# Expert weights: who computes the low half, VectorE behind its own share of a group, or ScalarE and GpSimd behind ScalarE's share

## The chip, the cores and the metric

One core of a Trainium2 chip runs the whole program. The metric is the device time of one execution in microseconds. Beside it the profiler records one execution instruction by instruction; where a text speaks of "the trace", it means that execution.

## What is computed

Three layers follow each other, cut here to what matters.

```python
# 1: attention through 32 packed tokens; batch 8, 8 heads, 576 tokens, head size 64
p_packed = softmax_attention(p, k, v)
x = softmax_attention(q, p_packed, p_packed)          # -> (8, 576, 512)
# 2: Fourier mixing, normalisation and a channel MLP
u = x + real(fft(fft(x, axis=1), axis=2))
x = u + relu(norm(u) @ w_ch1) @ w_ch2                 # 512 -> 2048 -> 512
# 3: mixture of 8 experts, each token goes to one of them
h = relu(x[b, s] @ w1[e])                             # 512 -> 1024
out[b, s] = p[e] * (h @ w2[e])                        # 1024 -> 512
```

The weights `w1` and `w2` come in 32-bit floats. The kernel multiplies in 16-bit floats: each operand is kept as a high half, the value rounded to 16 bits, and a low half, what the rounding lost, and a product is the sum of three passes (high by high, high by low, low by high).

## The kernel before, in words

The program goes through the batch with a software pipeline. `Mix` is the channel MLP of one batch element: 16 groups `f`. In a group, `mm1(f)` makes `hp` with 12 matmuls of 512 columns (L739), ScalarE takes the relu into the high half of `ht` (L746), VectorE makes its low half (L747), and two groups later `mm2` adds 12 more matmuls into `acc` (L759). This is the bulk of TensorE's work. Between the matmuls of a group `tick()` draws steps from background generators: the attention and Fourier part of the next batch element (`attention`, L315 on), the end of the last one (`after_mix`), and `expert_weights`. Two of the Mix runs, R0 and R1, have 256 columns. A scheduler fixes the order of each engine's queue when the program is built, and every engine runs its own queue strictly in that order; a step of the attention that comes late on any engine thus holds TensorE at the matmul that needs it.

`expert_weights` turns 64 blocks `st` (128 x 1024, named `se` in the trace, two buffers) into 128 tiles `so` (128 x 2 x 512, two buffers) of high and low halves and writes them to the scratch tensors `WS1` and `WS2`, from which the third layer loads them. Per tile, `split` scales into the high half on ScalarE (L261) and subtracts on VectorE (L262). SyncE's queue issues the load of `se` (L300) and the write of `so` (L309). This goes on from 176 to 962 us of the trace. `pace[0]` is VectorE's last instruction of the newest group (L747); `tc.issue_after(pace[0])` orders the instructions that the block puts on the same engine behind that one, and makes no wait on another engine.

The steps of attention that come up below, with their lines: `s` (L368), the first scores, in the accumulation buffers `att`, of which there are two; `scores2`, `greatest2` (L498, L500), the exponentials (L504), `sums2` on GpSimd (L509, L510), `divide2` on VectorE (L515 to L518), `fold2` (L525, L526, L530 to L534), `parts2` (`eh`, ScalarE L540, GpSimd L542, for the last third VectorE L544); `channels` k = 0 to 3, matmuls `gp` (L469) that ScalarE (L473) and VectorE (L474) turn into `g`. `lp` (L776), `bp` (L563) and `gp` take turns on the two `att` buffers, so the matmuls of one wait until VectorE has read an earlier one. At the end of a batch element `qs` (L632, ScalarE) and `rl`, `ru` (VectorE, L636 to L658) do the last 32 rows, and `s` of the next element takes the buffer that `ru` leaves. `un`, `unh` and a transposing DMA (L689 to L696) make the next Mix's operand.

Of the kernel before, what the change touches and what calls it, by code (L numbers as in the profile page):

```python
# [11 lines left out]
AF = mybir.ActivationFunctionType  # L12
ALU = mybir.AluOpType
# [140 lines left out]
def build(tc, A, stop=None, manual=False):  # L154
    nc = tc.nc
    with ExitStack() as ctx:
        if manual:
            ctx.enter_context(tc.manual_schedule())
        _build(tc, nc, ctx, A, stop)
# [20 lines left out]
def _build(tc, nc, ctx, A, stop):  # L180
# [72 lines left out]

    U, UT = {}, {}
    wdone = [0]
    pace = [None]
    held = []


    def split(dst_hi, dst_lo, src, scale):  # L260
        nc.scalar.activation(dst_hi, src, AF.Copy, scale=scale)  # L261
        nc.vector.scalar_tensor_tensor(dst_lo, src, scale, dst_hi, ALU.mult, ALU.subtract)  # L262
# [31 lines left out]
    def expert_weights():  # L294
        for e in range(NE):
            for k in range(8):

                st = wp.tile([128, 2, 512], F32, tag="st", name=f"se{e}_{k}", bufs=2)
                src = A["w1"][e, :, k] if k < 4 else A["w2"][e, :, 2 * k - 8:2 * k - 6].rearrange("p a n -> p (a n)")
                nc.sync.dma_start(st.rearrange("p a n -> p (a n)"), src)  # L300
                yield
                for a in range(2):
                    so = wp.tile([128, 2, 512], F16, tag="so", name=f"so{e}_{k}_{a}", bufs=2)

                    with tc.issue_after(pace[0]):
                        split(so[:, 0], so[:, 1], st[:, a], 64.0 if k < 4 else 256.0)
                    yield
                    c0 = 2048 * (k % 4) + 1024 * a
                    nc.sync.dma_start((WS1 if k < 4 else WS2)[e, :, c0:c0 + 1024], so.rearrange("p x n -> p (x n)"))  # L309
                yield  # L310
# [392 lines left out]
    def tick(n=1.0):  # L703
        for it in list(bg):
            if it[0] is ew and phase[0] < EWS:
                continue
            it[1] += it[2] * n
            while it[1] >= 1.0:
                it[1] -= 1.0
                try:  # L710
                    next(it[0])
                except StopIteration:
                    bg.remove(it)
                    break
# [9 lines left out]
    class Mix:  # L724
# [5 lines left out]
        def mm1(self, f):  # L730
            ntok, ut = self.ntok, self.ut
            phase[0] = f
            while wdone[0] <= f:
                next(cw)
            hp = psM.tile([128, 512], F32, tag="h", name=f"hp{self.tiles[0][1]}_{f}")
            n = 0
            for c in range(4):
                for (x, y) in PASS:
                    nc.tensor.matmul(hp[:, :ntok], w1h[:, f, c, x], ut[:, 4 * y + c, :ntok],  # L739
                                     start=n == 0, stop=n == 11)  # L740
                    n += 1
                if c < 3:
                    tick(ntok / 2048)
            ht = wp.tile([128, 2, 512], F16, tag="ht", name=f"ht{self.tiles[0][1]}_{f}", bufs=3)
            with tc.high_priority(offset=URGENT):
                nc.scalar.activation(ht[:, 0, :ntok], hp[:, :ntok], AF.Relu)  # L746
                pace[0] = nc.vector.scalar_tensor_tensor(ht[:, 1, :ntok], hp[:, :ntok], 0.0, ht[:, 0, :ntok],  # L747
                                                         ALU.max, ALU.subtract).ins
            self.hts[f] = ht
            tick(ntok / 2048)  # L750
# [282 lines left out]


    cw, ew = ch_weights(), expert_weights()
    for n, _ in enumerate(attention(0)):
        if n == CW0:
# [207 lines left out]
```

## Time and profile before

| what | value |
|---|---|
| median of three runs | 1516.62 us |
| lowest and highest | 1511.03 and 1521.59 us |
| the profiled execution | 1514.66 us |
| its span, first to last instruction | 1512.9 us |
| TensorE's mean granted clock | 0.971 of full speed |

Predictions start from the profiled execution and end at the median. In the rows of the profile PE is TensorE, DVE is VectorE, ACT is ScalarE, POOL is GpSimd and SP is SyncE; `out<-in` names what an instruction writes and reads, and after a bar stand busy time, the mean duration of one, and the idle time of the engine before it with what ended it.

### The profile page before, as it was taken

To read this page: it belongs to the slowest core of one execution; us is meant where nothing else is said; L and a number is where in the kernel's file an instruction comes from. 1 tells how busy PE (TensorE), PEld (TensorE's weight loads), DVE (VectorE), ACT (ScalarE), POOL (GpSimd) and SP (SyncE) were. 2 spreads that over 40 slices of the span, in tenths; PEclk is the share of its full clock that TensorE was granted. 3 is DMA by queue.
4 is the path that set the end of the run, shared out by engine and by line. 5 is a ranking of instruction groups with operands and counts; after the bars stand their busy time and mean duration, and the time that the engine had idled before them with its cause. 6 is when DMAs were issued, how large, how long until landed. Compare 5 with 4: busy or idle time off the path is not lost. (4 is left out here: it accounts for less than half of the span.)

```text
span 1512.9 us, 28826 instructions
## 1 busy us (share of the span) xinstructions
PE 1403.3 (93%) x11340; PEld 825.5 (55%) x11340; DVE 769.0 (51%) x1615; ACT 460.5 (30%) x858; POOL 278.9 (18%) x296
## 2 busy tenths in 40 slices
PE   4588888998999899999999999999899999999996
PEld 3334434544564454454444456455677677777764
DVE  5789977567655766666766665433531111111110
ACT  3343444344333434434435333111111111111111
POOL 1312113203200420320321220000212121121211
PEclk6689999999999999999999999999999999999998
DMA  8275476386476637647656546244946636783371
GB/s 268 61 226 177 142 190 156 111 208 164 122 166 158 191 108 201 170 118 219 149 131 198 125 124 170 56 180 139 252 114 197 170 89 172 226 245 81 79 230 54
DMA packets 233163, 239.70 MB, mean 158 GB/s; under 512 B 168191, under 2 KB 179583, under 8 KB 232384
## 3 DMA queue, kind: packets, MB, share of 16 engines
q1 hardware_dynamic: 226464, 217.62, 52.6%
q0 software_dynamic: 6560, 20.19, 4.1%
q8 instruction: 91, 1.49, 0.4%
q14 instruction: 48, 0.39, 0.1%
HBM read 267.38 MB, written 53.74 MB: 212 GB/s over the span
## 5 line engine op out<-in xcount | busy, mean ns | idle before, releaser
L759 PE MATMUL acc<-w2h,ht 128*128 128x512 f16 x1728 | 410.3, 379 | 0.8 <-DVE ul L767 0.8
L739 PE MATMUL hp<-ut,w1h 128*128 128x512 f16 x1536 | 371.3, 383 | 5.9 <-DMA ut<-unh 5.2
L739 PEld LDWEIGHTS <-w1h 128*128 128x128 f16 x1920 | 183.7, 98 | 187.8 <-issue 21.0
L759 PEld LDWEIGHTS <-ht 128*128 128x128 f16 x1728 | 165.7, 98 | 185.2 <-issue 6.6
L1107 PE MATMUL ehp<-xgt,w1b 128*128 128x128 f16 x3936 | 232.6, 219 | 3.3 <-DMA w1b<-WS 2.2
L1107 PEld LDWEIGHTS <-w1b 128*128 128x128 f16 x3936 | 225.2, 98 | 15.5 <-DMA w1b<-WS 2.6
L1115 DVE SCALAR_TENSOR_TENSOR hx<-ehp,hx 128x512 f16<-128x512 f32 x82 | 56.6, 691 | 339.3 <-ACT hx L1114 335.5
L1125 PE MATMUL eo<-w2b,hx 128*128 128x512 f16 x984 | 219.2, 379 | 0.0
L747 DVE SCALAR_TENSOR_TENSOR ht<-hp,ht 128x512 f16<-128x512 f32 (+1 forms) x160 | 101.3, 633 | 165.9 <-ACT ht L746 165.7
L1125 PEld LDWEIGHTS <-hx 128*128 128x128 f16 x984 | 94.3, 98 | 106.3
L261 ACT ACTIVATE so<-se 128x512 f16<-128x512 f32 x128 | 79.8, 628 | 194.6 <-DMA WS<-so 154.6
L746 ACT ACTIVATE ht<-hp 128x512 f16<-128x512 f32 (+1 forms) x160 | 87.2, 546 | 138.6 <-PE hp L739 133.5
L1114 ACT ACTIVATE hx<-ehp 128x512 f16<-128x512 f32 x82 | 48.9, 597 | 185.9 <-PE ehp L1107 185.9
L262 DVE SCALAR_TENSOR_TENSOR so<-se,so 128x512 f16<-128x512 f32 x128 | 98.2, 776 | 10.7 <-ACT so L261 10.7
L1133 POOL DMA_INDIRECT out<-ys,sidx x41 | 41.5, 1013 | 332.2 <-ACT ys L1132 310.8
L1132 ACT ACTIVATE ys<-eo,scl 128x512 f32<-128x512 f32 x41 | 28.2, 687 | 179.2 <-PE eo L1125 179.2
L344 POOL TENSOR_TENSOR qh<-q,qh 128x1420 f16<-128x1420 f32 x12 | 34.6, 2880 | 257.3 <-ACT qh L343 233.9
L1075 POOL DMA_INDIRECT xg<-XS,gidx x41 | 42.2, 1029 | 174.9 <-DVE sidx L1031 103.9
L368 PE MATMUL s<-k,p 64*32 64x288 f32 x256 | 24.3, 478 | 24.8 <-DVE ru L648 11.6
L739 PE MATMUL hp<-utr,w1h 128*128 128x256 f16 x384 | 47.1, 272 | 0.0
L563 PE MATMUL bp<-cst,eh 128*128 128x289 f16 (+1 forms) x192 | 33.5, 317 | 13.2 <-ACT eh L540 6.5
L694 POOL TENSOR_TENSOR unh<-un,unh 128x512 f16<-128x512 f32 x32 | 38.6, 1216 | 30.7 <-ACT unh L693 30.7
(288 smaller groups left out, 1346.4 us busy)
## 6 DMA issues: line engine op xcount, KB each, us to landing
w1b<-WS SPq DMA_DIRECT2D x156, 512.0 KB
w2b<-WS SPq DMA_DIRECT2D x156, 512.0 KB
se<-in_w SPq DMA_DIRECT2D x64, 512.0 KB
WS<-so SPq DMA_DIRECT2D x128, 256.0 KB
sw<-in_wc SPq DMA_DIRECT2D x32, 512.0 KB
q<-in_qd SPq DMA_DIRECT2D x16, 710.0 KB
v<-in_vd SPq DMA_DIRECT2D x16, 640.0 KB
k<-in_kd SPq DMA_DIRECT2D x16, 576.0 KB
```

The lines of the kernel that those rows point to most:

```text
L261: nc.scalar.activation(dst_hi, src, AF.Copy, scale=scale)
L262: nc.vector.scalar_tensor_tensor(dst_lo, src, scale, dst_hi, ALU.mult, ALU.subtract)
L739: nc.tensor.matmul(hp[:, :ntok], w1h[:, f, c, x], ut[:, 4 * y + c, :ntok], start=n == 0, stop=n == 11)
L746: nc.scalar.activation(ht[:, 0, :ntok], hp[:, :ntok], AF.Relu)
L747: pace[0] = nc.vector.scalar_tensor_tensor(ht[:, 1, :ntok], hp[:, :ntok], 0.0, ht[:, 0, :ntok], ALU.max, ALU.subtract).ins
L759: nc.tensor.matmul(self.acc[j], ht[:, x, 128 * j:128 * j + 128], w2h[:, f, y], start=f == 0 and n == 0, stop=f == 15 and n == 2)
L1075: nc.gpsimd.indirect_dma_start(out=g_, out_offset=None, in_=XS[0:rows], in_offset=bass.IndirectOffsetOnAxis(ap=gidx[:, b:b + 1], axis=0), ...
L1107: nc.tensor.matmul(hp[:, cols], w1b[b % RB][:, 2 * c + fg, x, cols], xt[b][:, 4 * y + c], start=n == 0, stop=n == 11, skip_group_check=True)
L1114: nc.scalar.activation(ht[:, fg, 0], hp, AF.Relu)
L1115: nc.vector.scalar_tensor_tensor(ht[:, fg, 1], hp, 0.0, ht[:, fg, 0], ALU.max, ALU.subtract)
L1125: nc.tensor.matmul(op, h[:, f // 4, x, 128 * (f % 4):128 * (f % 4) + 128], w2b[b % RB][:, f, y], start=n == 0, stop=n == 23)
L1133: nc.gpsimd.indirect_dma_start(out=A["out"], out_offset=bass.IndirectOffsetOnAxis(ap=sidx[:, b:b + 1], axis=0), in_=ys, in_offset=None, bo ...
```

## The change

For the 128 tiles `so` of the experts' weights the call of `split` is replaced by three instructions. ScalarE scales the 128 x 512 block of `st` in place, in 32 bits; ScalarE copies it into the high half; GpSimd subtracts the high half from the scaled block into the low half. VectorE has no part in it any more. The block is now ordered behind `pace[1]`, ScalarE's relu of the newest group, so ScalarE's two instructions stand behind that relu; GpSimd's one has no such order. `split` stays as it is for the other weights. Line numbers after the change are higher by 2 from there on.

```diff
-    pace = [None]
+    pace = [None, None]
...
-                    with tc.issue_after(pace[0]):
-                        split(so[:, 0], so[:, 1], st[:, a], 64.0 if k < 4 else 256.0)
+                    with tc.issue_after(pace[1]):
+                        nc.scalar.activation(st[:, a], st[:, a], AF.Copy, scale=64.0 if k < 4 else 256.0)
+                        nc.scalar.copy(so[:, 0], st[:, a])
+                        nc.gpsimd.tensor_tensor(so[:, 1], st[:, a], so[:, 0], op=ALU.subtract)
...
-                nc.scalar.activation(ht[:, 0, :ntok], hp[:, :ntok], AF.Relu)
+                pace[1] = nc.scalar.activation(ht[:, 0, :ntok], hp[:, :ntok], AF.Relu).ins
```

The first place is the softmax of attention 5 in groups 7 and 8. On VectorE, before, from the second `g` on (`m_5_2`, `ee_2`, `eo_2` belong to the last third of the rows, `gp_1` to `gp_3` are the channel products):

```order
L474 SCALAR_TENSOR_TENSOR g_6214<-gp_1_6420,g_6214 128x257
L515 TENSOR_REDUCE m_5_2_6354<-t_5_2_6410 99x16
L262 SCALAR_TENSOR_TENSOR so_3_1_6444<-se_3_6345,so_3_1_6444 128x512
L516 TENSOR_SCALAR m_5_2_6354<-m_5_2_6354 99x16
L517 RECIPROCAL m_5_2_6354<-m_5_2_6354 99x16
L518 TENSOR_TENSOR ee_2_6356<-ee_2_6356,m_5_2_6354 99x512
L532 SCALAR_TENSOR_TENSOR eo_2_6451<-ee_2_6356,c_93 99x256
L533 TENSOR_SCALAR eo_2_6451<-eo_2_6451,c_93 99x256
L526 SCALAR_TENSOR_TENSOR ah_2_6447<-ee_2_6356,ah_2_6447 32x512
L474 SCALAR_TENSOR_TENSOR g_6214<-gp_2_6464,g_6214 128x257
```

and after:

```order
L517 TENSOR_REDUCE m_5_2_6424<-t_5_2_6481 99x16
L518 TENSOR_SCALAR m_5_2_6424<-m_5_2_6424 99x16
L519 RECIPROCAL m_5_2_6424<-m_5_2_6424 99x16
L520 TENSOR_TENSOR ee_2_6426<-ee_2_6426,m_5_2_6424 99x512
L534 SCALAR_TENSOR_TENSOR eo_2_6523<-ee_2_6426,c_93 99x256
L528 SCALAR_TENSOR_TENSOR ah_1_6474<-ee_1_6362,ah_1_6474 128x512
L476 SCALAR_TENSOR_TENSOR g_6283<-gp_1_6491,g_6283 128x257
L535 TENSOR_SCALAR eo_2_6523<-eo_2_6523,c_93 99x256
L528 SCALAR_TENSOR_TENSOR ah_2_6519<-ee_2_6426,ah_2_6519 32x512
L546 SCALAR_TENSOR_TENSOR eh_2_6545<-eh_2_6545,c_93,eo_2_6523 99x512
L476 SCALAR_TENSOR_TENSOR g_6283<-gp_2_6536,g_6283 128x257
```

The two tiles `so` are gone from VectorE, and `g` of `gp_1` now stands behind the whole division of `ee_2` and behind `ah_1`; it stood ahead of it. On GpSimd the same stretch, before:

```order
L510 TENSOR_TENSOR t_5_2_6410<-t_5_2_6410 99x16x8
L542 TENSOR_TENSOR eh_0_6400<-eo_0_6383,eh_0_6400 128x512
L542 TENSOR_TENSOR eh_1_6429<-eo_1_6407,eh_1_6429 128x512
L534 TENSOR_TENSOR eo_2_6451<-ee_2_6356 99x256
L387 MEMSET ehl_0_7124 128x2x64
```

and after:

```order
L512 TENSOR_TENSOR t_5_2_6481<-t_5_2_6481 99x16x8
L544 TENSOR_TENSOR eh_0_6471<-eo_0_6453,eh_0_6471 128x512
L308 TENSOR_TENSOR so_3_0_6464<-se_3_6415,so_3_0_6464 128x512
L536 TENSOR_TENSOR eo_2_6523<-ee_2_6426 99x256
L544 TENSOR_TENSOR eh_1_6500<-eo_1_6478,eh_1_6500 128x512
L308 TENSOR_TENSOR so_3_1_6515<-se_3_6415,so_3_1_6515 128x512
```

A subtraction for `so` now stands behind each of the two `eh` instructions.

The second place is the end of attention 5, on ScalarE, where `qs_2` is copied, which `rl` and `ru` on VectorE need; before:

```order
L693 CAST unh_1_1_6875<-un_1_1_6873 128x512
L746 ACTIVATE ht_14_6896<-hp_14_6878 128x512
L261 ACTIVATE so_0_0_6957<-se_0_6944 128x512
L632 COPY qs_2_6929<-P_2_6899 32x257
L261 ACTIVATE so_0_1_6974<-se_0_6944 128x512
```

and after:

```order
L695 CAST unh_1_1_6954<-un_1_1_6952 128x512
L307 CAST so_7_1_6965<-se_7_6927 128x512
L748 ACTIVATE ht_14_6976<-hp_14_6957 128x512
L306 ACTIVATE se_0_7024<-se_0_7024 128x512
L634 COPY qs_2_7009<-P_2_6979 32x257
L307 CAST so_0_0_7037<-se_0_7024 128x512
```

Ahead of `qs_2` stood the making of a tile `so`; now the scaling of the loaded block stands there, and the copy of an earlier block stands ahead of `ht_14`. TensorE's own queue has the same instructions in both programs. In four batch elements the first scores `s` have moved ahead of two or three of the large matmuls beside them.

## Rows read from the trace of the kernel before

**Rows 1.** Page, part 1: engine, busy us, share of the span, instructions

```profile
PE 1403.3 (93%) x11340; PEld 825.5 (55%) x11340; DVE 769.0 (51%) x1615; ACT 460.5 (30%) x858; POOL 278.9 (18%) x296
```

**Rows 2.** One stretch: length, busy us (count) of PE, PEld, DVE, ACT, POOL; granted clock

```profile
176.00:962.00 786.00, 746.44 (x5067) 386.72 (x5065) 508.84 (x1044) 305.06 (x583) 160.00 (x156) 0.99 0.59 155
```

**Rows 3.** What TensorE waited for, 176 to 962 us: total us, times, longest

```profile
PE lp L776 <- DVE g L474: 8.0, 5, 2.0
PE s L368 <- issue: 7.1, 3, 2.6
PE bp L563 <- DVE g L474: 3.5, 4, 1.2
PE gp L469 <- DVE g L474: 2.9, 3, 1.2
PE s L491 <- ACT pth L448: 2.6, 1, 2.6
PE gp L469 <- DVE ee L500: 2.2, 2, 1.8
PE s L368 <- DVE ru L648: 2.1, 1, 2.1
PE pps L427 <- DVE vhl L416: 2.0, 2, 1.3
```

**Rows 4.** Groups of instructions, 176 to 962 us: busy us, mean ns, idle before

```profile
L262 DVE SCALAR_TENSOR_TENSOR so<-se,so 128x512 f16<-128x512 f32 x128 | 98.2, 776 | 10.7 <-ACT so L261 10.7
L747 DVE SCALAR_TENSOR_TENSOR ht<-hp,ht 128x512 f16<-128x512 f32 (+1 forms) x133 | 82.9, 623 | 131.2 <-ACT ht L746 131.0
L261 ACT ACTIVATE so<-se 128x512 f16<-128x512 f32 x128 | 79.8, 628 | 194.6 <-DMA WS<-so 154.6 <-DVE ee L500 6.4 <-issue 5.5
...
L694 POOL TENSOR_TENSOR unh<-un,unh 128x512 f16<-128x512 f32 x28 | 33.6, 1210 | 28.1 <-ACT unh L693 28.1
...
L504 ACT ACTIVATE ee<-ee 128x512 f32<-128x512 f32 (+1 forms) x18 | 11.2, 622 | 8.1 <-DVE ee L500 8.1
```

**Rows 5.** One line each, 176 to 962 us: duration ns min/median/max

```profile
L747 DVE SCALAR_TENSOR_TENSOR ht<-hp,ht x133: 411/684/693, 177.0 to 959.7; 128x512 f16<-128x512 f32 x101, 128x256 f16<-128x256 f32 x32
L526 DVE SCALAR_TENSOR_TENSOR ah<-ee,ah x18: 672/676/3161, 245.6 to 855.8; 128x512 f16<-128x512 f32 x12, 32x512 f16<-32x512 f32 x6
L516 DVE TENSOR_SCALAR m<-m x18: 131/174/1902, 242.9 to 851.3; 128x16 f32<-128x16 f32 x12, 99x16 f32<-99x16 f32 x6
```

**Rows 6.** VectorE's timeline, attention 5, groups 7 and 8: start us, duration us

```profile
630.05 0.42 DVE L474 SCALAR_TENSOR_TENSOR g<-gp,g 128x257 f16<-128x257 f32 x1
...
631.49 2.54 DVE L262 SCALAR_TENSOR_TENSOR so<-se,so 128x512 f16<-128x512 f32 x1
...
637.18 0.41 DVE L474 SCALAR_TENSOR_TENSOR g<-gp,g 128x257 f16<-128x257 f32 x1
```

**Rows 7.** GpSimd's timeline of the same stretch

```profile
631.21 2.27 POOL L542 TENSOR_TENSOR eh<-eo,eh 128x512 f16<-128x512 f32 x2
```

**Rows 8.** TensorE's timeline of the same stretch

```profile
633.06 0.52 PE L469 MATMUL gp<-cdt,pth 128*64 128x257 f16 x6
...
637.64 0.17 PE L776 MATMUL lp<-wgh,xt 128*128 128x18 f16 x1 [2.01 <-DVE g L474]
```

**Rows 9.** Timelines at the end of attention 5: ScalarE, VectorE, TensorE

```profile
679.92 0.63 ACT L261 ACTIVATE so<-se 128x512 f16<-128x512 f32 x1 [2.02 <-DMA WS<-so]
680.57 0.37 ACT L632 COPY qs<-P 32x257 f32<-32x257 f32 x1
...
680.58 0.69 DVE L262 SCALAR_TENSOR_TENSOR so<-se,so 128x512 f16<-128x512 f32 x1 [1.96 <-ACT so L261]
...
682.32 0.41 DVE L648 TENSOR_TENSOR ru<-P,qs 32x256 f32<-32x256 f32 x1
682.82 0.69 PE L368 MATMUL s<-k,p 64*32 64x288 f32 x8 [2.09 <-issue]
```


## Prediction

> **What bounds the kernel now.** The page comes first: TensorE is busy for 93% of the span, VectorE for 51%, ScalarE for 30% and GpSimd for 18% [rows 1]. No change to the other engines can win more than what TensorE waits for. The second look is at the stretch in which the expert weights are made, 176 to 962 us. Of its 786 us TensorE is busy for 746.4, so 39.6 us are idle; VectorE is the next fullest with 508.8 us, ScalarE has 305.1 and GpSimd 160.0. The clock there is 0.99 of full speed, so it has nothing to give back [rows 2]. The third look is at what those idle microseconds wait for. Matmuls that wait for VectorE take 8.0 + 3.5 + 2.9 + 2.2 + 2.1 + 2.0 = 20.7 us in 17 waits. Three waits of the first scores `s` have no named releaser and take 7.1 us, and one of them ends just after VectorE's `ru` (682.32 + 0.41 = 682.73 against 682.82), so they belong to VectorE too. ScalarE holds TensorE once, for 2.6 us [rows 3, 9]. The sum that this change can touch is thus 20.7 + 7.1 = 27.8 us in 20 waits. It is no single long wait: each is one to three microseconds, at a step of the attention that VectorE, in its fixed order, did late.
>
> **What leaves VectorE.** 128 subtractions of 776 ns in the mean, 98.2 us busy in all [rows 4], a fifth of VectorE's 508.8 us. Nearly all of that lies beside TensorE's work and is worth nothing by itself. Its worth is in the queue: where a subtraction stands between a late input and the instruction that TensorE waits for, the wait is shorter by its length. At the end of attention 5 one of 0.69 us stands just there, between `qs` and `rl` [rows 9]. One such in front of each of the 20 waits would give 20 x 0.69 = 13.8 us. This overstates it at the four `s` waits, since `s` itself now stands two or three large matmuls earlier in TensorE's queue, so that TensorE begins to wait earlier; it is too low where the subtraction was itself held, as the one of 2.54 us in groups 7 and 8 [rows 6]. I take half of it, **7 us** gained, with ends of 0 and 27.8.
>
> **What comes onto ScalarE.** The copy into the high half takes the place of the old scaling, 628 ns, at no cost. The scaling in place is new; the nearest row is the exponential in place on the same shape and 32-bit type, 622 ns [rows 4]. 128 x 0.622 = 79.6 us, so ScalarE goes from 305 to 385 of 786 us. What is queued behind these are the relus `ht`, `qs`, `g`, `eh` and `ah`. The relus have two groups of room: TensorE's list of waits has no matmul that waits for `ht` from ScalarE. At the end of attention 5 the scaling of `se_0` takes the place of the old making of `so_0_0` ahead of `qs_2`: 0.62 us for 0.63. But what it waits for is other: the old one waited until 679.92 for a write of `so` to land, the new one for the load of `se_0`, which can start only when GpSimd has read the block two before it. I count no gain there. Overall TensorE today waits 2.6 us for ScalarE with 305 us of load; in proportion to the load that grows by a quarter, 0.7 us. I take **1 us** lost, between 0 and 10 (a scaling of 0.62 us at each of some 16 of these places).
>
> **What comes onto GpSimd.** The nearest row is `unh`, the same subtraction on the same shape and types: 1210 ns [rows 4]. 128 x 1.21 = 154.9 us; GpSimd goes from 160 to 315 us of 786, from 0.20 to 0.40. The work as such fits. Behind it are queued `t`, `eo` and `eh` of the softmax, the norm's power and `unh`. And SyncE's writes of `so` wait for GpSimd instead of VectorE, with the transposing DMAs behind them in its queue. At 1.21 for 0.68 us a tile is finished about half a microsecond later, plus 0.62 for the scaling; a new tile is wanted every 786 / 128 = 6.1 us, so two buffers carry that.
>
> **What GpSimd's work does to VectorE.** This is the term that decides. The subtraction of 2.54 us on VectorE began at 631.49 and ended at 634.03; GpSimd's two `eh` ran from 631.21 to 633.48 [rows 6, 7]. Subtractions of this shape with both inputs in SBUF otherwise take 0.68 us (the median of `ah`, 676 ns), so this one stood still until GpSimd's run of two was over, and then took its usual time. The same shows in single lines: `ah`, with both inputs in SBUF, ranges from 672 to 3161 ns, and a small `tensor_scalar` of the softmax from 131 to 1902, while the relu's low half, which reads PSUM and has one input in SBUF, never exceeds 693 ns in 133 [rows 5]. So VectorE instructions of certain kinds wait out GpSimd's. The subtraction of `so` was one of the kind; its loss over 0.68 us, 128 x (0.776 - 0.68) = 12 us, goes with it. But the others meet twice as much of GpSimd. [...]
>
> Its price at the place where the profile shows it: in groups 7 and 8 of attention 5 the division of the last third (L515 to L518), `ah_1` and then `g` of `gp_1` now follow each other on VectorE, with a subtraction of `so` behind each `eh` on GpSimd. The first `g`, at 630.05 before, was ahead of all that. TensorE wanted `gp_3`, which needs that buffer, at 633.06, and then `lp` at 635.63, which it got at 637.64 [rows 6, 8]. If VectorE slips in between GpSimd's instructions, the division is done some 2.5 us sooner and 2 us of the wait are gone. If it stands until a run is over, `gp_3` waits some 5.7 us (worked out with the rival below). This happens once in each of the six batch elements 2 to 7, so the ends are 6 x (-2) = -12 (most of it already in the first term) and 6 x 3.5 = +21 us. I take 0.5 us a time, **3 us** lost, nearer to the middle because the run lengths before and after at the division itself are about equal (two `eh` before, 2.27 us; an `eh` and a subtraction after).
>
> **Sum.** -7 + 1 + 3 = -3 us. From the profiled 1514.66 this is 1511.7 us; the median of the runs is 1516.62, that is 1.96 above the profiled one, so the forecast is 1513.6 us. Within 1% (15 us) a measurement of this kernel cannot tell a time from no change.
>
> **Rival A, all of VectorE's waits go.** With a fifth of its load gone VectorE is on time everywhere, and GpSimd's longer runs fall into its pauses. For it: nearly all of TensorE's waits end on VectorE. [...] It gives 1516.6 - 26 = 1490, and half of it, 1503, joins the forecast's range.
>
> **Rival B, slower: GpSimd's runs shut VectorE out of the softmax.** Place: groups 7 and 8 of each of six batch elements. `eh_0` and the subtraction end at about 633.5, the division at 634.6; then `eo_2`, `eh_1` and the next subtraction run for 0.7 + 1.2 + 1.2 = 3.1 us, `ah_1` follows at 637.7 and `g` of `gp_1` ends at 638.8. `gp_3` starts 5.7 us late, and `lp`, behind nine large matmuls (2.0 us) and the rest of VectorE's chain, at 641.2 in place of 637.64: 3.5 us, six times, 21 us. With 4 us saved elsewhere that is 1516.6 + 17 = 1534. It decides from the point at which `gp` L469 waits over 3 us for `g` in most batch elements.
>
> **Rival C, ScalarE stalls on its own tiles.** ScalarE already idles for 154.6 us until writes of `so` have landed [rows 4]. A longer chain through GpSimd lengthens each of those waits, in a queue that holds `qs`, `g` and `eh`. At 10 us lost, the upper end of ScalarE's term, and 3 us at the port against a gain of 7, it gives 1522.6.
>
> **How the numbers follow.** The forecast, 1505 to 1521, has a chance of 0.5; A 0.2, B 0.2, C 0.1. Faster by over 1% (under 1501.5) comes from A, with a little from the forecast: 0.2. Slower by over 1% (over 1531.8) is most of B: 0.18. The rest is 0.62. The range cuts A and B about in half, 1496 to 1533.
>
> **What would show it.** VectorE's busy time in the stretch should fall by 70 to 98 us and no `so` be left on it; ScalarE's should rise by about 80 and GpSimd's by about 155. The waits of `lp` and `bp` for `g` should fall and those of `gp` for `g` rise; `ah`, `eo` and the small `tensor_scalar` should have longer means. If the sum of TensorE's waits in 176 to 962 us stays between 30 and 42 us, the steps were right. If the waits for VectorE fall under 10 us, the first term was too small; if new ones on GpSimd or on the `so` writes take over 15 us, the chain through GpSimd was underrated.

## The result and the profile after

The changed kernel takes 1497.38 us, the median of four runs (1495.18 to 1500.60), against 1514.63 us for the kernel before in four runs (1511.03 to 1521.59). The ratio is 0.989, with a 95% interval of 0.986 to 0.992: 17 us less, faster by 1.1%. The profiled execution took 1495.18 us, with a span of 1493.4.

The page of the kernel after, part 1, answers to [rows 1]:

```profile
PE 1398.4 (94%) x11340; PEld 823.3 (55%) x11340; DVE 709.6 (48%) x1487; ACT 525.1 (35%) x986; POOL 418.0 (28%) x424
```

The stretch in which the expert weights are made, kernel after, answers to [rows 2]; the columns are the length, the busy time of PE, PEld, DVE, ACT and POOL with their counts, the granted clock, and the DMA's share and rate:

```profile
176.00:962.00 786.00, 757.49 (x5148) 391.73 (x5147) 455.99 (x936) 370.88 (x713) 299.03 (x284) 0.98 0.59 157
```

The work went where it was meant to go. VectorE is busy for 456.0 us in place of 508.8, ScalarE for 370.9 in place of 305.1, GpSimd for 299.0 in place of 160.0. TensorE's idle time in this stretch fell from 39.6 to 786 - 757.5 = 28.5 us, and the stretch holds 81 more of its matmuls than before. So the gain lies here, but the engine totals do not say by which edit.

What TensorE waited for in the same stretch, kernel after, answers to [rows 3]; total us, times, longest:

```profile
PE gp L471 <- DVE g L476: 16.4, 5, 4.5
PE pps L429 <- DMA et<-ehl: 2.6, 1, 2.6
PE gp L471 <- DVE ee L502: 2.1, 1, 2.1
...
PE lp L778 <- DVE g L476: 1.6, 1, 1.6
...
PE bp L565 <- DVE g L476: 0.5, 1, 0.5
```

Two things are to be seen. Every wait of `s` is gone: in [rows 3] there were 7.1 + 2.1 = 9.2 us at the first scores (L368) and 2.6 us at the second ones (L491), 11.8 us in all. `lp` and `bp` wait for `g` for 2.1 us in place of 11.5. Against that `gp` waits for `g` for 16.4 us in place of 2.9, and one wait alone takes 4.5 us. The kernel gained at several steps of the attention and lost mainly at one, the softmax in groups 7 and 8.

Groups of instructions in the stretch, kernel after, answer to [rows 4] (`L306` the scaling, `L307` the copy, `L308` the subtraction); busy us, mean ns, idle before with what ended it:

```profile
L308 POOL TENSOR_TENSOR so<-se,so 128x512 f16<-128x512 f32 x128 | 149.3, 1171 | 269.4 <-ACT so L307 251.1 <-DMA XS<-xh 8.5 <-issue 8.5
...
L307 ACT CAST so<-se 128x512 f16<-128x512 f32 x128 | 77.8, 615 | 13.0 <-DMA WS<-so 9.8
L306 ACT ACTIVATE se<-se 128x512 f32<-128x512 f32 x128 | 77.5, 622 | 0.2
...
L518 DVE TENSOR_SCALAR m<-m 128x16 f32<-128x16 f32 (+1 forms) x18 | 17.5, 971 | 0.6
...
L534 DVE SCALAR_TENSOR_TENSOR eo<-ee,c 99x256 f32<-99x256 f32 x6 | 13.9, 2309 | 0.6
```

The durations of the new instructions are as the nearest rows had them (622 ns for 622, 1171 for 1210). The number that was not foreseen stands behind the second bar of `L307`. Before, ScalarE sat idle for 154.6 us in front of its `so` instruction until a write of `so` had landed [rows 4]; now that is 9.8 us. The price of the move shows in the last two lines: the small `tensor_scalar` `m` takes 971 ns in the mean, and `eo` of the last third 2309. The same two groups before:

```profile
L516 DVE TENSOR_SCALAR m<-m 128x16 f32<-128x16 f32 (+1 forms) x18 | 7.6, 421 | 0.4
L532 DVE SCALAR_TENSOR_TENSOR eo<-ee,c 99x256 f32<-99x256 f32 x6 | 6.2, 1034 | 0.7
```

### The profile page after: what moved, and what is told of

It is laid out like the page before. It is cut to its first block, busy times and chain, and to the rows that moved or that the text cites. A ratio compares the mean times of both kernels' runs of the same rounds, so it can differ in the third digit from the quotient of the medians.

```text
span 1493.4 us, 28983 instructions
## 1 busy us (share of the span) xinstructions
PE 1398.4 (94%) x11340; PEld 823.3 (55%) x11340; DVE 709.6 (48%) x1487; ACT 525.1 (35%) x986; POOL 418.0 (28%) x424
## 5 line engine op out<-in xcount | busy, mean ns | idle before, releaser
L761 PE MATMUL acc<-w2h,ht 128*128 128x512 f16 x1728 | 417.0, 383 | 0.0
L308 POOL TENSOR_TENSOR so<-se,so 128x512 f16<-128x512 f32 x128 | 149.3, 1171 | 269.4 <-ACT so L307 251.1
L307 ACT CAST so<-se 128x512 f16<-128x512 f32 x128 | 77.8, 615 | 13.0 <-DMA WS<-so 9.8
L306 ACT ACTIVATE se<-se 128x512 f32<-128x512 f32 x128 | 77.5, 622 | 0.2
```

Source lines behind the costliest of these rows:

```text
L306: nc.scalar.activation(st[:, a], st[:, a], AF.Copy, scale=64.0 if k < 4 else 256.0)
L307: nc.scalar.copy(so[:, 0], st[:, a])
L308: nc.gpsimd.tensor_tensor(so[:, 1], st[:, a], so[:, 0], op=ALU.subtract)
L761: nc.tensor.matmul(self.acc[j], ht[:, x, 128 * j:128 * j + 128], w2h[:, f, y], start=f == 0 and n == 0, stop=f == 15 and n == 2)
```

## The experiments

Three theories were to be told apart. **Theory 1**, the prediction's own: the gain comes from what left VectorE. **Theory 2**, its rival: it comes from the order alone, `pace[1]` in place of `pace[0]`, which puts the making of `so` behind ScalarE's relu and, as it was expected, no longer ahead of `qs`. **Theory 3** is on the loss in the softmax: GpSimd's subtractions read SBUF and shut VectorE out while they do; its rival is that VectorE's order alone makes `g` late, since `g` of `gp_1` now stands behind the division.

Where times of different experiments are set side by side, they are taken by their ratios to the kernel before, which ran beside each of them, times 1514.6 us. These can differ by a microsecond or two from the differences of the medians, and each interval is some 3 to 7 us wide to either side.

### The order alone

Against the kernel before:

```diff
-    pace = [None]
+    pace = [None, None]
...
-                    with tc.issue_after(pace[0]):
+                    with tc.issue_after(pace[1]):
                         split(so[:, 0], so[:, 1], st[:, a], 64.0 if k < 4 else 256.0)
...
-                nc.scalar.activation(ht[:, 0, :ntok], hp[:, :ntok], AF.Relu)
+                pace[1] = nc.scalar.activation(ht[:, 0, :ntok], hp[:, :ntok], AF.Relu).ins
```

> The kernel before, with the tiles ordered behind ScalarE's relu (pace[1]) instead of VectorE's low half of it, and everything still computed by split on ScalarE and VectorE. Theory 1 (the gain comes from the subtraction leaving VectorE's queue): no gain, 1508 to 1520 us, and the waits of lp, bp and s in 176 to 962 us stay above 15 us together. Theory 2 (the gain comes from ScalarE's tiles standing behind the relu and no longer ahead of qs): 1495 to 1503 us.

Measured: 1487.70 us, ratio 0.983 (0.979 to 0.987), 24 us less than the 1512.12 beside it. No instruction is added or removed, VectorE still does all 128 subtractions, and the kernel is faster than the changed one. The group `L261` of this kernel in the stretch, columns as above:

```profile
L261 ACT ACTIVATE so<-se 128x512 f16<-128x512 f32 x128 | 78.0, 622 | 5.5 <-DMA WS<-so 5.1
```

What its TensorE waited for there, the two longest rows:

```profile
PE bp L563 <- DVE g L474: 6.4, 5, 1.7
PE lp L776 <- DVE g L474: 4.7, 5, 1.4
```

ScalarE's idle time for the writes of `so` falls from 154.6 to 5.1 us, in 7 waits for 85, and the waits of `s` are gone here too, but for one of 0.4 us. What is left are short waits for `g`. Theory 1 falls: the waits of `lp`, `bp` and `s` are 11.5 us together, and the time is far under its 1508 us. Theory 2 is right that the order alone makes the gain, but the time is lower than its 1495 to 1503 us too, and its reason needs mending, as the next rows show.

From the 17th to the 144th relu `ht`, with the same matmuls between them (203.6 to 951.1 us of the trace before, 202.9 to 926.9 of this one), the time falls by 23.5 us and TensorE's idle time from 37.9 to 18.9. The four waits of the first scores are 9.2 us of these 19.0; the rest is spread over shorter waits, which were not followed one by one.

The end of attention 5 shows how. ScalarE, VectorE, TensorE and SyncE in this experiment, start us and duration, to be set beside [rows 9]:

```profile
657.81 0.60 ACT L746 ACTIVATE ht<-hp 128x512 f16<-128x512 f32 x1 [0.15 <-PE hp L739]
658.31 0.62 ACT L261 ACTIVATE so<-se 128x512 f16<-128x512 f32 x1
658.96 0.37 ACT L632 COPY qs<-P 32x257 f32<-32x257 f32 x1
...
659.05 0.68 DVE L262 SCALAR_TENSOR_TENSOR so<-se,so 128x512 f16<-128x512 f32 x1
659.76 0.42 DVE L636 TENSOR_TENSOR rl<-P,qs 32x256 f32<-32x256 f32 x1
...
661.28 0.69 PE L368 MATMUL s<-k,p 64*32 64x288 f32 x8
...
655.70 0.34 SPq L309 DMA_DIRECT2D WS<-so  x1
```

ScalarE's row of `so` is the same as in [rows 9], and it stands in the same place, between `ht` and `qs`. Only the 2.02 us of waiting for a write are missing. VectorE's `so` stands ahead of `rl` as it did before, and `s` waits for nothing: the 0.69 us on VectorE that the prediction priced were not what held it. At another of the four waits, 2.58 us at 571.78 in the kernel before, no `so` of VectorE stood there at all, and VectorE was idle for ScalarE:

```profile
570.27 0.41 DVE L636 TENSOR_TENSOR rl<-P,qs 32x256 f32<-32x256 f32 x1 [3.19 <-ACT qs L632]
```

The write that `so` needs went out at 655.70. In the kernel before, SyncE's timeline has it here:

```profile
676.20 1.24 SPq L696 DMA_TRANSPOSE ut<-unh  x1
677.53 1.00 SPq L309 DMA_DIRECT2D WS<-so  x2
```

There it stood behind a transposing DMA that went out only at 676.20. It followed at 677.53, and `so` started at 679.92, 2.39 us later. The same distance from 655.70 gives, as an estimate, 658.09, 0.22 us before ScalarE wanted the buffer. SyncE's order in the two programs, before and in this experiment:

```
L300 DMA se_0_6944<-in_w 128x1024
L696 DMA_TRANSPOSE ut_6694<-unh_1_0_6860 128x8x128
L309 DMA WS_126<-so_7_0_6866 128x1024
L309 DMA WS_126<-so_7_1_6886 128x1024
L696 DMA_TRANSPOSE ut_6694<-unh_1_1_6875 128x8x128
```

```
L300 DMA se_0_6944<-in_w 128x1024
L309 DMA WS_126<-so_7_0_6866 128x1024
L696 DMA_TRANSPOSE ut_6694<-unh_1_0_6860 128x8x128
L696 DMA_TRANSPOSE ut_6694<-unh_1_1_6875 128x8x128
L309 DMA WS_126<-so_7_1_6886 128x1024
```

So the edit has put both `so_7` tiles behind `ht_13` on ScalarE, where `so_7_0` stood ahead of `ht_12` and `so_7_1` ahead of `ht_13`, and the first one's write ahead of the transposing DMA on SyncE. With that the wait of `so_0_0`, which needs the buffer of `so_7_0`, has gone. So it is not that `so` left the place ahead of `qs`: at three of the four places it still stands there, and only its wait is missing. All four show the same course. Before, two writes go out behind a transposing DMA (at 299.50, 565.99, 677.53 and 787.28), ScalarE sits for 1.97 to 2.31 us ahead of `so`, `qs` follows, and the first scores wait for 2.09 to 2.58 us. With the order alone, the first write goes out about 1 us ahead of the transposing DMA each time (at 291.32, 547.67, 655.70 and 762.12), and neither ScalarE nor the first scores wait there.

The changed kernel gets rid of the same wait in another way. Its ScalarE and SyncE at that place:

```profile
667.90 0.63 ACT L306 ACTIVATE se<-se 128x512 f32<-128x512 f32 x1
668.55 0.37 ACT L634 COPY qs<-P 32x257 f32<-32x257 f32 x1
669.94 0.62 ACT L307 CAST so<-se 128x512 f16<-128x512 f32 x1 [1.02 <-DMA WS<-so]
...
667.50 0.52 SPq L311 DMA_DIRECT2D WS<-so  x1
```

The write is behind a transposing DMA again (issued at 666.16) and lands 2.4 us later, but what stands ahead of `qs` is the scaling, which writes `se` and needs no `so`. The 1.02 us of waiting for the write are still there, behind `qs`, where they hold nobody.

### No order at all

Against the kernel after; the second one is the same edit of the kernel before, at `pace[0]`:

```diff
-                    with tc.issue_after(pace[1]):
+                    with nullcontext():
```

> The changed kernel without any ordering of the tiles (issue_after taken away), so ScalarE's scaling and copy may stand ahead of the relu. Theory 1: the time stays near the changed kernel, 1493 to 1504 us. Theory 2: the gain is lost, 1508 us or more.

> The kernel before with no order at all for the tiles (issue_after(pace[0]) taken away). Theory 2 (ScalarE's order decides): VectorE's order behind its low half is not worth much, ScalarE's is free in both, so the time is within 15 us of the kernel before, 1505 to 1530 us. If an order on any engine is what holds the tiles back, it is far worse, 1550 us or more, as with the changed kernel without order (1574.7 us).

Measured: without its order the changed kernel takes 1574.66 us, ratio 1.042 (1.038 to 1.047), and the kernel before 1538.77 us, ratio 1.014 (1.009 to 1.019). Theory 2 is borne out by the first (1508 us or more). The second misses its range of 1505 to 1530 us: it is 23 us over the kernel before beside it, so the order behind VectorE's low half was worth more than was thought. The tiles are then made early and in a rush: in the second, the last instruction of `L261` starts at 581.9 us in place of 946.9. ScalarE's idle time for the writes is 116.4 us in the second, and TensorE waits 12.2 us for `ht` and once 10.8 us for the scaling in the first. The changed block has no instruction on VectorE, so behind `pace[0]` it would have had no order either. By the ratios the order is worth 22 us to the kernel before and 81 to the changed one, so most of what the changed kernel's three instructions could cost is held back by the line that puts them behind the relu.

### The subtraction back on VectorE

Against the kernel after:

```diff
-                        nc.gpsimd.tensor_tensor(so[:, 1], st[:, a], so[:, 0], op=ALU.subtract)
+                        nc.vector.tensor_tensor(so[:, 1], st[:, a], so[:, 0], op=ALU.subtract)
```

> The changed kernel with its scaling in place and its order behind ScalarE's relu, but with the subtraction on VectorE again. Theory 1: as slow as the kernel before or slower, 1512 to 1530 us, since VectorE has its 128 instructions back and ScalarE has 80 us more. Theory 2: 1495 to 1503 us.

Measured: 1488.65 us, ratio 0.983 (0.979 to 0.988). This kernel differs from the order alone by the extra scaling on ScalarE, whose busy time in the stretch is 373.1 us against 303.8, and in time by 0.95 us, which is within the intervals. ScalarE's extra work costs nothing that could be measured. Theory 1 (1512 us or more) falls here too, and again the time is under the 1495 to 1503 us of theory 2, which had no price for GpSimd's part. From the changed kernel it differs by the engine of the subtraction, and it is 8.7 us faster; its highest run is 1489.73 us and the changed kernel's lowest 1495.18. So with this order, taking the subtraction from VectorE to GpSimd is a loss of 8 to 9 us by itself.

### What in GpSimd's part costs: memsets, a second subtraction

Against the kernel after, two memsets of the same tile in place of the subtraction:

```diff
-                        nc.gpsimd.tensor_tensor(so[:, 1], st[:, a], so[:, 0], op=ALU.subtract)
+                        nc.gpsimd.memset(so[:, 1], 0.0)
+                        nc.gpsimd.memset(so[:, 1], 0.0)
```

And the subtraction twice:

```diff
                         nc.gpsimd.tensor_tensor(so[:, 1], st[:, a], so[:, 0], op=ALU.subtract)
+                        nc.gpsimd.tensor_tensor(so[:, 1], st[:, a], so[:, 0], op=ALU.subtract)
```

> The changed kernel with the subtraction replaced by two memsets of the low half to zero on GpSimd: the low halves of the experts' weights are left out. VectorE's order is the same, GpSimd writes and reads nothing from SBUF for these tiles. Theory 3 (the new waits of gp for g, 16.4 us, come from GpSimd's subtraction shutting VectorE out while it reads SBUF): those waits fall under 6 us and the time to 1480 to 1490 us. Its rival (they come from VectorE's order alone, g of gp_1 now standing behind the division): they stay over 11 us, time 1493 to 1500 us.

> The changed kernel with GpSimd's subtraction for each tile done twice, 128 x 1.17 us more on GpSimd and nothing else changed. If GpSimd's length is what costs the changed kernel some 9 us against the same order with the subtraction on VectorE (1488.7 us), then as much again or more: 1505 to 1520 us, with longer VectorE instructions where both inputs lie in SBUF. If GpSimd's work is hidden and only VectorE's order costs: 1494 to 1501 us.

Measured: with memsets 1494.52 us, ratio 0.989 (0.985 to 0.993), which is not to be told from the changed kernel. With the second subtraction 1527.40 us, ratio 1.007 (1.005 to 1.009), 28 us over the changed kernel by the ratios, more than the 1505 to 1520 us that were expected. TensorE's longest row of waits in the stretch, with memsets:

```profile
PE gp L472 <- DVE g L477: 13.6, 5, 3.3
```

The same with two subtractions:

```profile
PE gp L472 <- DVE g L477: 23.2, 6, 5.7
```

Memsets read nothing, and yet `gp` waits 13.6 us for `g`, not under 6. The expectation from theory 3 is missed, and waits and time lie where its rival had them: memsets in place of the subtraction take away only 16.4 - 13.6 = 2.8 us of these waits. The two memsets take about as long as the subtraction (0.52 us each against 1.15), so they do not tell what GpSimd's length and place cost. The place in attention 5 shows why. VectorE and then GpSimd, with memsets:

```profile
616.80 1.72 DVE L519 TENSOR_SCALAR m<-m 99x16 f32<-99x16 f32 x1
...
619.72 2.15 DVE L535 SCALAR_TENSOR_TENSOR eo<-ee,c 99x256 f32<-99x256 f32 x1
...
616.87 1.16 POOL L545 TENSOR_TENSOR eh<-eo,eh 128x512 f16<-128x512 f32 x1
617.97 0.52 POOL L309 MEMSET so<- 128x512 f16 x1
...
620.44 1.15 POOL L545 TENSOR_TENSOR eh<-eo,eh 128x512 f16<-128x512 f32 x1
621.53 0.52 POOL L308 MEMSET so<- 128x512 f16 x1
```

`m` ends at 618.52, just behind the memset at 618.49; so a memset holds it too. `eo`, with two inputs in SBUF, ends at 621.87, behind `eh` (621.59) and not behind the memset that follows (622.05). With the real subtraction both are held to the end of it: in the kernel after, `m` ends at 619.25 with the subtraction ahead of it at 619.22, and `eo` at 623.70 with the one at 623.42. Why the memset held `m` and not `eo`, no run here shows. But `eh_1` now comes between `eo` and its end with either filling, since GpSimd's order has put `eh_1` behind `eo_2`: `eo` takes 2.15 us here with memsets and 3.25 with the subtraction, against 1.03 in the mean before, so about half of what came on top is there with memsets too. Whether VectorE's order alone would do it is what the next edit asks.

### `g` ahead of the division

Against the kernel after, and the same against the order alone:

```diff
-            nc.vector.scalar_tensor_tensor(g[:, hf, 1, cs], gp[:, :257], 1.0, g[:, hf, 0, cs],
-                                           ALU.mult, ALU.subtract)
+            gi[k] = nc.vector.scalar_tensor_tensor(g[:, hf, 1, cs], gp[:, :257], 1.0, g[:, hf, 0, cs],
+                                                   ALU.mult, ALU.subtract).ins
...
         def divide2(i):
+            with tc.issue_after(gi[1]) if i == 2 else nullcontext():
+                nc.vector.tensor_reduce(m2[:, 1], m2s[i, 1][:, :, :8], axis=AX.X, op=ALU.add)
...
```

> The changed kernel with one edge more: on VectorE the division of the last third (divide2(2)) stands behind g of gp_1. If VectorE's order makes the 16.4 us of gp waiting for g, these fall under 5 us and the time to 1483 to 1490 us. [...]

> The kernel with split kept and the tiles behind ScalarE's relu (1487.7 us), with the same edge on VectorE. There gp waits only 2.3 us for g, and lp and bp 11 us for g of gp_2 and gp_3, which the edge does not put earlier: 1484 to 1491 us, no clear gain; a gain of over 5 us would say that g's place counts there too.

Measured: on the changed kernel 1494.80 us, ratio 0.986 (0.981 to 0.991); on the order alone 1484.06 us, ratio 0.980 (0.975 to 0.984), the lowest median of all. In the first, `gp` waits for `g` for 5.9 us in place of 16.4, but `lp` for 5.0 and `bp` for 2.3: `g` no longer stands behind the division, it now stands behind `ah_1`. VectorE and GpSimd in attention 5 of that kernel:

```profile
618.11 4.89 DVE L531 SCALAR_TENSOR_TENSOR ah<-ee,ah 128x512 f16<-128x512 f32 x1 [0.98 <-ACT ah L530]
622.92 0.41 DVE L478 SCALAR_TENSOR_TENSOR g<-gp,g 128x257 f16<-128x257 f32 x1
...
617.96 1.16 POOL L547 TENSOR_TENSOR eh<-eo,eh 128x512 f16<-128x512 f32 x1
619.07 1.16 POOL L308 TENSOR_TENSOR so<-se,so 128x512 f16<-128x512 f32 x1
620.19 1.15 POOL L547 TENSOR_TENSOR eh<-eo,eh 128x512 f16<-128x512 f32 x1
621.30 1.15 POOL L308 TENSOR_TENSOR so<-se,so 128x512 f16<-128x512 f32 x1
```

`ah_1` takes 4.89 us in place of 0.68: it stands until GpSimd's run of four, without a gap from 617.96 to 622.45, is over. Changing the order on VectorE moved the victim here, from `eo` to `ah_1`: GpSimd's run stayed, and another instruction was in front of it. The waits of `gp`, 5.9 us, stay over the 5 us, and the time stays over the 1483 to 1490 us, that were expected if VectorE's order makes them: that order alone is not the cause. On the order alone the same edit takes the waits of `gp` for `g` away without this; the time lies at the lower end of the 1484 to 1491 us expected, and the 3.6 us between the two medians (5 by the ratios) are within the intervals.

### No tiles in the softmax

Against the kernel after, and the same against the fastest above:

```diff
-EW_RATE = 1.3
+EW_RATE = 1.65
...
-            if it[0] is ew and phase[0] < EWS:
+            if it[0] is ew and (phase[0] < EWS or 6 <= phase[0] <= 8):
```

> The changed kernel with no tiles drawn in groups 6 to 8 of a Mix, and the other groups drawing 1.65 instead of 1.3 steps, so that no subtraction stands between eh and eo on GpSimd in the softmax. If the place of GpSimd's subtractions is what costs the changed kernel its 9 us against VectorE doing them: gp waits for g fall under 6 us and the time to 1485 to 1491 us. If their mere number costs (GpSimd twice as busy everywhere): 1494 to 1500 us.

> The best so far (split kept, tiles behind ScalarE's relu, division behind g of gp_1, 1484.1 us) with the same holes in groups 6 to 8. VectorE loses the subtractions that still stand in the softmax there; lp and bp wait for g 11 us in all. If these go: 1474 to 1481 us. If the denser drawing in the other groups makes new waits there, 1483 us or more.

Measured: 1486.46 us, ratio 0.982 (0.979 to 0.985), and 1484.31 us, ratio 0.981 (0.978 to 0.985). The first keeps all 128 subtractions on GpSimd and makes no tile in groups 6 to 8. Its waits of `gp` for `g` in the stretch:

```profile
PE gp L471 <- DVE g L476: 0.4, 2, 0.2
```

Its group of `eo`:

```profile
L534 DVE SCALAR_TENSOR_TENSOR eo<-ee,c 99x256 f32<-99x256 f32 x6 | 5.0, 827 | 0.0
```

The 16.4 us of `gp` are 0.4 us now, `eo` is back at 827 ns, and the kernel is 11 us faster than the changed one with the same work on every engine: GpSimd is busy for 298.8 us in the stretch, as after (299.0). So it is not how much GpSimd does, it is beside what. On the fastest kernel, which has nothing of this kind on GpSimd, the same edit leaves the time as it was, not at the 1474 to 1481 us hoped for. That is a sum of two changes: its waits of `lp` and `bp` for `g` fall from 11.2 to 4.8 us, and new ones come, `pps` for `vhl` from 0.5 to 4.9 us and the first scores from none to 3.8. That the closer tiles in the other groups make these is likely, but not shown.

## Why the prediction was right, and where it was wrong

The time of 1497.38 us lies in the range, 1.4 us above its lower end, and outside the forecast's own 1505 to 1521. The forecast was 3 us less; it became 17. That the range holds it is luck: it reaches down to 1496 for the sake of rival A, in which VectorE is on time everywhere, and that is not what happened. Being faster by over 1%, as it came, had been given a chance of 0.2. One mechanism was left out of the sum and one term was too small, on opposite sides, and the two errors partly cancelled. By the ratios, at 1514.6 us:

| step | in the sum, us | measured, us | from |
|---|---|---|---|
| the order behind ScalarE's relu | none ("I count no gain there") | -25.7 | the order alone (0.983) |
| ScalarE's extra scaling | +1 (0 to 10) | +0.6 | subtraction on VectorE (0.9834) against the order alone |
| VectorE relieved | -7 (-27.8 to 0) | -2.4 | no tiles in the softmax (0.9818) against subtraction on VectorE |
| GpSimd beside VectorE in the softmax | +3 (-12 to +21) | +10.9 | the change (0.989) against no tiles in the softmax |
| sum | -3 | -16.6 | the change by its own ratio: -16.7 |

The four measured steps are differences along one chain of kernels, so that they add up to the whole says nothing for them. The second and third are smaller than their intervals and not told apart from nothing. That no tiles are made in three groups also moves the other tiles; in the last experiment this came out even, but as a gain and a loss, so the third and fourth steps can be off by what it does here.

**The step that failed** is the one on ScalarE at the end of attention 5. The prediction had the row in its hand: 154.6 us in which ScalarE sat ahead of `so` until a write landed [rows 4], and one such wait of 2.02 us right ahead of `qs`, with `s` on TensorE late behind it [rows 9]. It saw that the scaling takes the place of the old `so` there and waits for a load in place of a write, and counted no gain, giving as the reason that the load too can start only late. It asked what the new instruction waits for, and not what TensorE gains when the old wait goes. The trace after shows the scaling at 667.90 with no wait at all, and 0.2 us of waiting before all 128 of them. Rival C even read the 154.6 us as a risk that would grow; they fell to 9.8.

**With it fell the attribution of the waits.** The first part put 27.8 us of TensorE's waits down to VectorE's queue, because VectorE was the releaser that the trace named. At the four waits of the first scores VectorE's chain `rl`, `ru` was itself waiting for ScalarE's `qs`, which stood behind `so`, which stood behind a write. The order alone removes them with VectorE's 128 subtractions in place. That VectorE's relief is worth little shows in the kernel with no tiles in the softmax: it has VectorE relieved and no loss at GpSimd, and it is as fast as the two that leave the subtraction on VectorE (1486.46 against 1488.65 and 1487.70). (Rival A counts 26 us for all of VectorE's waits, where the prediction's own sum of them is 27.8; it does not say why.)

**The term on GpSimd had the place and the mechanism, and too small a size:** 3 us where the table has 10.9. Rival C's sum puts these 3 us "at the port"; no run shows a port. What the runs showed is VectorE instructions held beside GpSimd's: in the kernel after, `m` takes 971 ns in the mean in place of 421, and `eo` of the last third 2309 in place of 1034. VectorE, GpSimd and TensorE in attention 5, groups 7 and 8, kernel after, answer to [rows 6 to 8]:

```profile
617.35 1.90 DVE L518 TENSOR_SCALAR m<-m 99x16 f32<-99x16 f32 x1
...
620.45 3.25 DVE L534 SCALAR_TENSOR_TENSOR eo<-ee,c 99x256 f32<-99x256 f32 x1
...
624.23 0.41 DVE L476 SCALAR_TENSOR_TENSOR g<-gp,g 128x257 f16<-128x257 f32 x1
...
616.95 1.16 POOL L544 TENSOR_TENSOR eh<-eo,eh 128x512 f16<-128x512 f32 x1
618.07 1.15 POOL L308 TENSOR_TENSOR so<-se,so 128x512 f16<-128x512 f32 x1
620.48 0.73 POOL L536 TENSOR_TENSOR eo<-ee 99x256 f32<-99x256 f32 x1 [1.26 <-DVE ee L520]
621.17 1.15 POOL L544 TENSOR_TENSOR eh<-eo,eh 128x512 f16<-128x512 f32 x1
622.27 1.15 POOL L308 TENSOR_TENSOR so<-se,so 128x512 f16<-128x512 f32 x1
...
624.70 0.86 PE L471 MATMUL gp<-cdt,pth 128*64 128x257 f16 x6 [4.54 <-DVE g L476]
```

This is rival B's course nearly word for word: `m` is held until the first run ends (619.22), `eo` until the second does (623.42), `ah_1` and `g` follow, and `gp_3` starts 4.5 us late, where 5.7 had been worked out. The one thing that differs is that `eo`, not `ah_1`, is the one that stands. The waits of this kind are 4.5 us and less, over 3 us in four of the six batch elements. Rival B's point of decision was reached, and its price at 6 x 3.5 = 21 us was still too high: some 11 us. Its time of 1534 did not come, for that reason and because ScalarE's order paid 26 us at the same time. The middle value of 3 us was taken because the run lengths at the division were about equal; the second run, behind `eo`, is what the sum passed over.

**What was to show it.** VectorE's busy time fell by 52.9 us in the stretch, not by 70 to 98: the 98.2 us of subtractions went, but `m` and `eo` alone grew by 18 x 0.55 + 6 x 1.28 = 17.6 us, others grew too, and the stretch now holds 20 more of VectorE's other instructions (936 against 1044 - 128). ScalarE's rose by 65.8 in place of 80, GpSimd's by 139.0 in place of 155. The waits of `lp` and `bp` fell and those of `gp` rose, as foretold; the listed waits of TensorE sum to about 28 us, just under the 30 to 42 that were to say that the steps were right. Most of these signs came although the largest step was missing: fewer waits of `lp` and `bp` fit theory 1 as well as theory 2, and only the runs with the order alone and with the subtraction back on VectorE tell the two apart. Within 15 us a time could not be told from no change, the prediction said; the interval of the ratio, 0.3% to either side, is some 5 us.

Two questions stay open. The wait for the write was taken away by order, not by more buffers; no run has more than two `so` buffers, and so it is not shown whether the wait alone, with the old order, accounts for all 26 us. And the second subtraction cost 28 us, more than the first did. TensorE's idle time in the stretch grew from 28.5 to 786 - 736.6 = 49.4 us with it, 6.8 us of that in the waits of `gp` for `g` and 4.9 in those of `pps` for `vhl`; why doubling costs so much more was not taken further.

## What to carry to other kernels

Before an engine is relieved, look for what its own releaser was waiting for: a wait that the trace puts down to VectorE began here at an instruction on ScalarE, which sat for 1.97 to 2.31 us ahead of `qs` until a write had landed, because the write stood in a third queue, SyncE's, behind a transposing DMA. One line of order that lets the write go out first was worth 24 us here, more than the whole change, with no work moved and `so` in most places still ahead of the urgent `qs`. When a change moves work and order at once, price the two apart, and measure the order alone first. GpSimd's work beside VectorE's was priced here by its place: the same 128 subtractions cost 8 to 9 us when they fell between the softmax's own GpSimd instructions, and nothing measurable, all in all, when they were kept out of three groups.

## What the runs showed of the hardware that was not expected

In three rows here a VectorE instruction that met a run of GpSimd instructions was held until the run was over, not until the instruction that it met was: 4.89 us for `ah` in front of four in a row and 3.25 us for `eo` in front of three, where two in a row cost 2.54 us before [rows 6, 7].

One stall of TensorE cost more than its length. The granted clock of the kernel after around the wait of 4.54 us, in stretches of 2 us (columns as above):

```profile
623.00:625.00 2.00, 0.30 (x4) 0.30 (x5) 2.00 (x5) 0.02 (x1) 0.43 (x1) 0.54 0.00 0
625.00:627.00 2.00, 2.00 (x10) 0.68 (x7) 1.86 (x4) 1.97 (x5) 0.00 (x0) 0.50 0.71 137
627.00:629.00 2.00, 2.00 (x6) 0.72 (x5) 0.74 (x2) 0.81 (x2) 1.24 (x2) 0.50 0.73 191
629.00:631.00 2.00, 2.00 (x18) 1.11 (x17) 0.41 (x2) 0.00 (x0) 0.11 (x1) 0.75 0.85 264
```

TensorE is idle from 624.70 - 4.54 = 620.16 us on. The granted clock, 1.00 from 616 to 622, is 0.50 from 625 to 629, 0.75 in the next stretch and 1.00 again from 631 to 633. The matmuls are longer there: six of `gp` take 0.86 us, where an earlier six took 0.52, and six of `acc` 2.74 us, where the six right before the wait took 1.46. While TensorE works again, an estimate from these rows is that 2 x 0.50 + 2 x 0.50 + 2 x 0.25 = 2.5 us of full-speed work are lost on top of the 4.5. Not every stall here was followed by this: in the kernel before, the clock stayed at 1.00 after the waits of 2.10, 2.09 and 2.39 us of the first scores (at 304.81, 682.82 and 792.69), and fell, to 0.55 between 573 and 575, after the one of 2.58 us at 571.78. In the whole stretch the mean granted clock is 0.98 in the kernel after, and 1.00 in the fastest kernel, none of whose waits for `g` is longer than 2.0 us.
